# One more tile transposed on TensorE, and two loads of v moved within GpSimd's queue, in a fused retention and snake-MLP kernel

## Chip, cores and metric

The kernel runs on one core of a Trainium2 chip. The metric is the device time of one execution in microseconds (us). Before the change it is 214.4 us, the median of three runs (214.03, 214.40, 214.58).

## What is computed

There are two stages. The first is a retention recurrence over q, k and v, each 4 sequences x 8 heads x 768 positions x 64. Each head has a state of 64 x 64:

```
state = gamma[h] * state + outer(k[t], v[t])
y[t]  = (1/8) * q[t] @ state
```

Its output, as 3072 rows of 512, is the input x of the second:

```
h   = x @ w_in                         # 512 -> 2048
g   = h + sin(alpha*h)**2 / alpha
out = g @ w_out                        # 2048 -> 512
```

## The kernel before

**Tiles.** Time is cut into chunks of 128 positions, so that there are 24 tiles of 128 rows, six to a sequence. The list `P` (`order`, lines 47 and 48) is the order in which they are computed: first the first chunk of each of the four sequences (P[0] to P[3], also called e0 to e3), then the rest of sequence 0 (P[4] to P[8]), of sequence 1 (P[9] to P[13]), of 2 and of 3. From P[10] on tiles are "wide": their q, k and v come not in a chunk of their own but with all wide tiles of their sequence, in eight loads a tensor, one for each head (`load_seq`, line 89). P[4] to P[9] have loads of their own (`load_chunk`, line 73).

**What one tile needs.** (1) Its q and k in SBUF, and from them the transposed tile `qkT`. `stage_T` (line 236) makes it with eight transposes on TensorE into a PSUM tile and a copy out on VectorE or ScalarE. `turn` (line 248) makes it with one transposing DMA on SP's queue. (2) `stage_A`, for wide tiles `scores`: TensorE makes q·k scores from `qkT` in the PSUM buffer of the tag `pa`, of which there is one, and VectorE masks them. (3) `stage_M`, for wide tiles `inter` and `mix` (both called by `burst`): scores times v, plus q times the state, plus the new state. The v must have been scaled by decay factors (`scale_v`, line 133), for most tiles on GpSimd. (4) The result, one column block of `xT`, feeds the MLP.

**The MLP.** Tiles are taken in groups: four, then ten groups of two. In a `Slot` TensorE multiplies two of the 16 blocks of w_in with a group's `xT` into a PSUM tile `ph` (line 420, tag `mm`, four buffers), ScalarE takes the sine (423) and mostly the square (428), VectorE adds both into `gT` (435). `ff_out` (line 442) multiplies `gT` of the group before with w_out (445), `take` copies the result out of PSUM and SP stores it (460).

**Order of the work.** It is written out by hand; each engine takes its instructions in the order of the program. Up to line 742 it is a list of calls: the first group's MLP with tiles P[4], P[5] and the transposes of P[6] in between. Then `phase` (line 558) runs phases 1 to 10, one for each later group, eight slots each. In each slot it first issues the slot's products, then the attention steps that a table has for this place, then a share of the group before. A place is (phase, slot): `score` and `blend` say where a tile's scores and its mix are issued, `turns` where its transposing DMA is. Places matter to SP only as the order of its queue: an instruction there waits for its own data and holds all that come behind it.

**GpSimd's queue** (lines 629 to 658) holds the loads of q, k and v, which change fp32 to bf16 on the way, and the scalings of v, in the order of the text. A load also waits, before it is issued, for the landing of the one issued eight places before. The scaling of a tile stands behind all loads above it, and waits for its own load.

Of the kernel before, what the change touches and what calls it, by code (L numbers as in the profile page):

```python
# [15 lines left out]
def kernel(  # L16
# [15 lines left out]
    nc = tc.nc  # L32
# [3 lines left out]
    NJ = B * NCH  # L36
# [32 lines left out]
    def chunk_of(t, j):  # L69
        b, c = divmod(j, NCH)  # L70
        return t[b, :, c * C:(c + 1) * C, :].rearrange("h s d -> s h d")

    def load_chunk(j, names="qkv"):
        for name, src in (("q", q), ("k", k), ("v", v)):
            if name not in names:
                continue
            if name == "v":
                t = big.tile([128, H, D], BF16, name="vr", tag="vr", bufs=10)
            else:
                if ("qk", j) not in raw:  # L80
                    raw["qk", j] = big.tile([128, 2, H, D], BF16, name="qkr", tag="qkr", bufs=9)
                t = raw["qk", j][:, "qk".index(name)]
            nc.gpsimd.dma_start(out=t, in_=chunk_of(src, j))  # L83
            raw[name, j] = t

    def wide(j):
        return j >= NCH + 2 and j % NCH > 0

    def load_seq(bt, names="qkv"):

        cs = [c for c in range(NCH) if wide(bt * NCH + c)]
        nh = 2 * len(cs)
        if "q" in names:
            raw["seq", bt] = (big.tile([128, nh, 2, NP, D], BF16, name=f"qk_seq{bt}"),
                              big.tile([128, nh, NP, D], BF16, name=f"v_seq{bt}"))
        tqk, tv = raw["seq", bt]
        for name, src in (("q", q), ("k", k), ("v", v)):
            if name not in names:
                continue
            for h in range(H):  # L100
                r = slice(64 * (h // NP), 64 * (h // NP) + 64)
                o = tv[r, :, h % NP, :] if name == "v" else tqk[r, :, "qk".index(name), h % NP, :]
                nc.gpsimd.dma_start(out=o, in_=src[bt, h, cs[0] * C:, :].rearrange("(f i) d -> i f d", i=64))  # L103
        for i, c in enumerate(cs):
            j, f = bt * NCH + c, slice(2 * i, 2 * i + 2)
            raw["qk", j], raw["k", j], raw["v", j] = tqk[:, f], tqk[:, f, 1], tv[:, f]
# [26 lines left out]
    def scale_v(j, eng):  # L133
        t, by = raw["v", j], kg
        if wide(j):
            t, by = t.rearrange("i f p d -> i (f p) d"), kgq
        eng.tensor_mul(t, t, by[:, j % NCH, :, None].to_broadcast([128, H, D]))  # L137
# [98 lines left out]
    def stage_T(j, eng=None, tag="ty"):  # L236
        pt = psum.tile([128, 2 * NP, 128], BF16, name="pt", tag=tag, bufs=4 if tag == "mm" else 1)
        st["qkT", j] = work.tile([128, 2 * NP, 128], BF16, name="qkT", tag="qkT", bufs=6)
        for i in range(2):
            for p in range(NP):  # L240
                nc.tensor.transpose(pt[:, i * NP + p, :],
                                    raw["qk"[i], j][:, 2 * p:2 * p + 2, :].rearrange("p h d -> p (h d)"), ident)
        if eng is nc.scalar:
            nc.scalar.copy(st["qkT", j], pt)
        else:
            nc.vector.tensor_copy(st["qkT", j], pt)
# [36 lines left out]
    def stage_M(j, tag="ty"):  # L283
        c = j % NCH
        g, i = place[j]
        if g not in xT:
            xT[g] = work.tile([128, KS, sizes[g] * C], BF16, name="xT", tag="xT", bufs=3)
        qkT, aT, vs = st["qkT", j], st["aT", j], raw["v", j]
        py = psum.tile([128, NP, 128], F32, name="py", tag=tag)
        if c > 0:  # L290
            for p in range(NP):
                for e in range(2):
                    r = slice(64 * e, 64 * e + 64)
                    nc.tensor.matmul(py[r, p, :], s_bd[c % 2][:, p, r], qkT[:, p, :],
                                     start=(p == 0), stop=True, skip_group_check=True)
        for p in range(NP):
            for e in range(2):
                nc.tensor.matmul(py[64 * e:64 * e + 64, p, :], vs[:, 2 * p + e, :], aT[:, e, p, :],  # L298
                                 start=(c == 0 and p == 0), stop=True, skip_group_check=True)
        x = xT[g][:, :, i * C:(i + 1) * C]  # L300
        if c == 0:
            nc.scalar.copy(x, py)
            return
        ps = stage_S(j) if c < NCH - 1 else None
        nc.vector.tensor_mul(x, py, qg[:, c])
        if ps is not None:
            keep_S(j, ps)
# [187 lines left out]
    P = order  # L495
    e0, e1, e2, e3 = P[:B]
# [133 lines left out]
    load_chunk(P[8], "qk")  # L630
    load_chunk(P[7], "v")
    load_chunk(P[9], "qk")
    scale_v(P[6], nc.gpsimd)
    load_seq(1, "q")
    load_chunk(P[8], "v")
    scale_v(P[7], nc.gpsimd)
    load_chunk(P[9], "v")
    load_seq(1, "k")
    scale_v(P[8], nc.gpsimd)
    scale_v(e1, nc.gpsimd)  # L640
    scale_v(P[9], nc.gpsimd)
    load_seq(1, "v")
    scale_v(e2, nc.gpsimd)
# [96 lines left out]
    F(2, 11, 16)  # L740
    stage_M(P[5])
    stage_T(P[6], nc.vector, "mm")
    score = {6: (1, 1), 7: (1, 4), 8: (2, 0), 9: (2, 2), 10: (2, 5)}
    blend = {6: (1, 4), 7: (1, 6), 8: (2, 2), 9: (2, 5)}
    for g in range(3, NG - 1):
        first = P.index(groups[g + 1][0])
        for i, n in enumerate((1, 5)):
            score[first + i + 1] = blend[first + i] = (g, n)
    turns = {7: (1, 0), 8: (1, 2), 9: (1, 4), 10: (2, 0), **{n + 2: score[n] for n in range(9, NJ - 2)}}
    atts = {g: {} for g in range(1, NG)}  # L750

    def at(place, fn):
# [61 lines left out]
```

## Time and profile before

| | |
|---|---|
| median of the runs shown | 214.4 us |
| profiled execution | 214.89 us |
| its span, first to last instruction | 213.1 us |
| TensorE (PE) busy | 202.5 us, 95% |
| ScalarE (ACT) busy | 159.2 us, 75% |
| VectorE (DVE) busy | 154.3 us, 72% |
| GpSimd (POOL) busy | 110.7 us, 52% |
| chain that ended last | PE 64%, DMA 21%, POOL 9% |
| granted TensorE clock | 1.0 |

The profile is of one execution; its times are counted from the span's first instruction. PE is the matrix products, PEld the loading of their stationary operand, which runs beside them. Products overlap each other and their ends are modelled, so where a piece of work ends is best read from where the next one starts. An instruction's idle time is that of its engine just before it, with what ended it. A DMA is told by its issue and by the time from there to its landing. The chain of work that ended last is followed back from the last instruction to whatever released each one.

### The profile page before, as it was taken

How to read it: one execution, taken by the hardware profiler on the slowest of the kernel's cores; microseconds unless marked ns; L12 is line 12 of the kernel's file. 1: busy time of each engine (PE TensorE's matmuls, PEld its weight loads, DVE VectorE, ACT ScalarE, POOL GpSimd, SP SyncE). 2: the span in 40 equal slices, each digit the busy share in tenths (PEclk: the TensorE clock that was granted, in tenths of full speed). 3: DMA queues.
4: the chain of work that ended last, by engine and by line, in shares of the span. 5: the costliest groups of instructions: out<-in, count | busy, mean ns of one | idle time of the engine just before them, and what ended most of it. 6: DMA issues, size and time to landing. Idle time of an engine off the chain costs nothing.

```text
span 213.1 us, 5488 instructions
## 1 busy us (share of the span) xinstructions
PE 202.5 (95%) x2187; PEld 132.9 (62%) x2187; DVE 154.3 (72%) x350; ACT 159.2 (75%) x343; POOL 110.7 (52%) x148
## 2 busy tenths in 40 slices
PE   7758999999799999999999999999999999999994
PEld 2324644567566666766767667667667667666654
DVE  7589994876878678678678777777877877666550
ACT  6687898457688867977977977977876876788821
POOL 8899433896869839899989931001231131000000
PEclk9999999999999999999999999999999999999999
DMA  9999999999999999999999994407403100110112
GB/s 131 145 176 182 206 208 178 154 201 168 145 148 105 130 157 142 171 92 183 169 142 156 150 141 104 98 3 98 103 11 92 51 30 23 52 49 0 49 52 98
DMA packets 101337, 25.00 MB, mean 117 GB/s; under 512 B 93872, under 2 KB 98368, under 8 KB 101312
## 3 DMA queue, kind: packets, MB, share of 16 engines
q0 software_dynamic: 77504, 13.38, 87.5%
q1 hardware_dynamic: 23664, 11.22, 25.7%
q8 instruction: 17, 0.28, 0.6%
q14 instruction: 8, 0.07, 0.1%
q10 hardware_dynamic: 144, 0.07, 0.1%
HBM read 27.27 MB, written 6.29 MB: 157 GB/s over the span
## 4 chain that ended last, share of the span: by engine, by line
PE 64%; DMA 21%; POOL 9%; DVE 2%; ACT 2%; issue 1%; SPq 0%; POOLq 0%; DVEq 0%
PE po L445 30%; PE ph L420 27%; DMA w_out<-in_moe_w_out_dram 8%; DMA vr<-in_v_dram 4%; DMA qkr<-in_k_dram 4%; POOL qkr L83 3%; DMA qkT<-qk_seq 3%; DMA qk_seq<-in_k_dram 2%; PE poh L470 2%; POOL vr L83 2%; PE pa L332 2%; PE py L322 1%; ACT dec L164 1%; POOL w_out L116 1%; POOL qg L208 1%
## 5 line engine op out<-in xcount | busy, mean ns | idle before, releaser
L435 DVE SCALAR_TENSOR_TENSOR gT<-s,rec_alpha,ph 128x256 bf16<-128x256 f32 (+3 forms) x184 | 82.0, 488 | 38.0 <-ACT s L428 37.8
L423 ACT ACTIVATE s<-ph,alpha_sb 128x256 f32<-128x256 f32 (+3 forms) x184 | 79.3, 480 | 33.8 <-PE ph L420 32.2
L420 PE MATMUL ph<-xT,w_in 128*128 128x256 bf16 (+3 forms) x736 | 98.8, 277 | 0.7 <-DMA w_in<-in_moe_w_in_dram 0.4
L445 PE MATMUL po<-w_out,gT 128*128 128x512 bf16 x368 | 95.2, 380 | 0.2 <-DMA w_out<-in_moe_w_out_dram 0.2
L420 PEld LDWEIGHTS <-w_in 128*128 128x128 bf16 x736 | 70.6, 98 | 31.3 <-DMA w_in<-in_moe_w_in_dram 1.3
L428 ACT ACTIVATE s<-s 128x512 f32<-128x512 f32 (+1 forms) x91 | 56.4, 623 | 2.6
L445 PEld LDWEIGHTS <-gT 128*128 128x128 bf16 x368 | 34.0, 98 | 26.0 <-issue 0.5
L386 POOL CAST s_bd<-s_f 64x256 bf16<-64x256 f32 x10 | 4.0, 396 | 41.7 <-DVE s_f L379 23.6
L137 POOL TENSOR_TENSOR v_seq<-v_seq,kgq 128x512 bf16<-128x512 bf16 x14 | 14.7, 1070 | 10.5 <-DMA v_seq<-in_v_dram 5.5
L103 POOL DMA_DIRECT2D qk_seq<-in_k_dram x24 | 17.0, 730 | 3.1 <-DMA vr<-in_v_dram 1.4
L103 POOL DMA_DIRECT2D qk_seq<-in_q_dram x24 | 17.1, 743 | 2.6 <-DMA qkr<-in_k_dram 0.9
L457 DVE COPY o_sb<-po 128x512 f32<-128x512 f32 x19 | 13.1, 692 | 5.9 <-PE po L445 5.9
L103 POOL DMA_DIRECT2D v_seq<-in_v_dram x24 | 17.0, 752 | 0.0
L341 DVE TENSOR_TENSOR aTw<-pa,maskq 128x768 bf16<-128x768 f32 x14 | 13.3, 950 | 0.0
L83 POOL DMA_DIRECT2D vr<-in_v_dram x10 | 9.3, 929 | 3.3 <-DMA w_out<-in_moe_w_out_dram 3.0
L372 DVE TENSOR_TENSOR xT<-py,qg 128x256 bf16<-128x256 f32 x28 | 10.5, 416 | 0.0
L83 POOL DMA_DIRECT2D qkr<-in_k_dram x9 | 8.0, 887 | 4.0 <-DMA w_out<-in_moe_w_out_dram 3.2
L83 POOL DMA_DIRECT2D qkr<-in_q_dram x9 | 8.1, 898 | 3.8 <-DMA w_in<-in_moe_w_in_dram 3.7
L137 POOL TENSOR_TENSOR vr<-vr,kg 128x512 bf16<-128x512 bf16 x8 | 8.5, 1074 | 0.8 <-PE py L298 0.8
L489 PE MATMUL spare<-warm 128*128 128x512 bf16 x18 | 7.2, 521 | 1.2 <-DVE warm L147 1.2
L264 DVE TENSOR_TENSOR aT<-pa,mask 128x1024 bf16<-128x1024 f32 x6 | 7.3, 1220 | 0.9 <-PE pa L260 0.8
L281 ACT CAST s_bd<-ps 64x256 bf16<-64x256 f32 x14 | 5.1, 362 | 2.0 <-PE ps L274 1.9
(94 smaller groups left out, 151.8 us busy)
## 6 DMA issues: line engine op xcount, KB each, us to landing
out_dram<-o_sb SPq DMA_DIRECT2D x23, 256.0 KB, 2.9
w_in<-in_moe_w_in_dram POOLq DMA_DIRECT2D x4, 512.0 KB, 9.5
w_out<-in_moe_w_out_dram POOLq DMA_DIRECT2D x4, 512.0 KB, 13.0
vr<-in_v_dram POOLq DMA_DIRECT2D x10, 128.0 KB, 7.2
qk_seq<-in_q_dram POOLq DMA_DIRECT2D x16, 80.0 KB, 6.0
qk_seq<-in_k_dram POOLq DMA_DIRECT2D x16, 80.0 KB, 4.6
v_seq<-in_v_dram POOLq DMA_DIRECT2D x16, 80.0 KB, 6.1
qkr<-in_q_dram POOLq DMA_DIRECT2D x9, 128.0 KB, 7.2
```

The source lines that it names most:

```text
L83: nc.gpsimd.dma_start(out=t, in_=chunk_of(src, j))
L103: nc.gpsimd.dma_start(out=o, in_=src[bt, h, cs[0] * C:, :].rearrange("(f i) d -> i f d", i=64))
L137: eng.tensor_mul(t, t, by[:, j % NCH, :, None].to_broadcast([128, H, D]))
L264: nc.vector.tensor_mul(aT.rearrange("p e n t -> p (e n) t"), pa.rearrange("p e n t -> p (e n) t"), m)
L341: return {"mask": lambda: nc.vector.tensor_mul(aT, pa[:, :, 0:384].rearrange("p e (m t) -> p e m t", m=2), maskq[:, None, None, :].to_broa ...
L372: nc.vector.tensor_mul(x[:, 2 * b:2 * b + 2, :], py[b][:, 0:256].rearrange("p (m t) -> p m t", m=2), qg[:, c, 2 * b:2 * b + 2])
L420: nc.tensor.matmul(self.ph[:, m, :], w_in[:, i, f * 128:(f + 1) * 128], xT[g][:, i, self.lo:self.hi], start=(m == 0 and i == 0), stop=(i = ...
L423: nc.scalar.activation(out=self.s[:, m, :], in_=self.ph[:, m, :], func=ACTF.Sin, scale=alpha_sb[:, f:f + 1])
L428: nc.scalar.activation(out=self.s, in_=self.s, func=ACTF.Square)
L435: nc.vector.scalar_tensor_tensor(gT[self.g][:, f, self.lo:self.hi], self.s[:, m, :], rec_alpha[:, f:f + 1], self.ph[:, m, :], op0=ALU.mult ...
L445: nc.tensor.matmul(po[g, ts], gT[g][:, f, ts * C:(ts + 1) * C], w_out[:, f, :], start=(f == 0), stop=(f == FF - 1))
L457: nc.vector.tensor_copy(o_sb, po[g, ts])
```

## The change

P[7]'s `qkT` is made by `stage_T` on TensorE, right behind P[6]'s, into the PSUM buffer `pa`, with the copy out on ScalarE; its transposing DMA at place (1, 0) goes. Those of P[8] and P[9] move to (1, 0) and (1, 2), and P[10]'s from (2, 0) to (1, 7), which puts it ahead of the store of the first group's last tile on SP. In GpSimd's queue P[8]'s v is loaded ahead of P[6]'s scaling and of sequence 1's q; the scalings of P[7], e1 and P[8] follow that q, ahead of sequence 1's k; P[9]'s v is loaded behind this k, and its scaling comes next, ahead of sequence 1's v. The number of loads and scalings is the same.

```diff
     load_chunk(P[8], "qk")
     load_chunk(P[7], "v")
     load_chunk(P[9], "qk")
+    load_chunk(P[8], "v")
     scale_v(P[6], nc.gpsimd)
     load_seq(1, "q")
-    load_chunk(P[8], "v")
     scale_v(P[7], nc.gpsimd)
+    scale_v(e1, nc.gpsimd)
+    scale_v(P[8], nc.gpsimd)
+    load_seq(1, "k")
     load_chunk(P[9], "v")
-    load_seq(1, "k")
-    scale_v(P[8], nc.gpsimd)
-    scale_v(e1, nc.gpsimd)
     scale_v(P[9], nc.gpsimd)
     load_seq(1, "v")
     scale_v(e2, nc.gpsimd)
...
     stage_M(P[5])
     stage_T(P[6], nc.vector, "mm")
+    stage_T(P[7], nc.scalar, "pa")
...
-    turns = {7: (1, 0), 8: (1, 2), 9: (1, 4), 10: (2, 0), **{n + 2: score[n] for n in range(9, NJ - 2)}}
+    turns = {8: (1, 0), 9: (1, 2), 10: (1, 7), **{n + 2: score[n] for n in range(9, NJ - 2)}}
```

## The prediction

> **What bounds the kernel now.** I read the busy time of the engines by stretches first (us, then busy us of PE, PEld, DVE, ACT, POOL; clock; DMA):
>
> ```profile
> 45.00:55.00 10.00, 9.62 (x117) 6.80 (x115) 6.60 (x13) 7.70 (x18) 8.31 (x12) 1.00 1.95 176
> 55.00:65.00 10.00, 8.82 (x94) 6.21 (x95) 7.78 (x15) 7.66 (x19) 7.46 (x11) 1.00 2.45 148
> 65.00:75.00 10.00, 9.48 (x122) 6.35 (x121) 7.21 (x15) 8.27 (x19) 8.65 (x12) 1.00 1.29 119
> 75.00:85.00 10.00, 10.00 (x115) 6.86 (x114) 7.95 (x18) 6.71 (x15) 6.68 (x9) 1.00 1.12 145
> 85.00:200.00 115.00, 115.00 (x1343) 79.69 (x1341) 84.93 (x197) 91.91 (x195) 46.85 (x65) 1.00 0.85 91
> ```
>
> TensorE (PE) is never idle from 75 to 200 us, at the full granted clock, so whatever moves it at 75 us moves the end. In the 30 us before, it idles 0.38 + 1.18 + 0.52 = 2.08 us: all that this change can reach. TensorE's timeline says where (start, us, what, idle before it and what ended that):
>
> ```profile
> 46.62 0.62 PE L241 MATMUL pt<-ident,qkr 128*128 128x128 bf16 x8
> 47.42 0.38 PE L420 MATMUL ph<-xT,w_in 128*128 128x256 bf16 x2 [0.18 <-DVE xT L305]
> ...
> 54.51 0.29 PE L274 MATMUL ps<-vr,qkr 128*64 128x64 bf16 x8
> 56.18 0.40 PE L260 MATMUL pa<-qkT 64*128 64x128 bf16 x8 [1.38 <-DMA qkT<-qkr]
> ...
> 73.47 0.29 PE L274 MATMUL ps<-vr,qkr 128*64 128x64 bf16 x8
> 74.28 0.25 PE L332 MATMUL pa<-qkT 64*64 64x128 bf16 x4 [0.52 <-DMA qkT<-qk_seq]
> ```
>
> The 1.38 us are the scores of the eighth tile, P[7], which wait for its transposing DMA. The 0.52 us are the scores of P[10], the first wide tile; SP's timeline shows both transposes in its queue:
>
> ```profile
> 41.59 5.39 SPq L460 DMA_DIRECT2D out_dram<-o_sb  x3
> 47.16 8.63 SPq L251 DMA_TRANSPOSE qkT<-qkr  x3
> 63.48 0.34 SPq L460 DMA_DIRECT2D out_dram<-o_sb  x1
> 68.27 2.90 SPq L251 DMA_TRANSPOSE qkT<-qk_seq  x2
> ```
>
> P[7]'s is issued at 47.16, behind three stores, and lands 9.0 later (DMA issues of that stretch), 56.1. P[10]'s must wait for the sequence's last k head, as the chain of waits tells; above it, what GpSimd (POOL) did:
>
> ```profile
> 53.27 8.97 DMA vr<-in_v_dram
> 62.24 0.28 issue
> 62.52 0.68 POOL qk_seq L103
> 63.20 0.21 issue
> 63.41 4.55 DMA qk_seq<-in_k_dram
> ...
> 68.27 5.97 DMA qkT<-qk_seq
> ```
>
> ```profile
> 64.11 3.05 POOL L137 TENSOR_TENSOR vr<-vr,kg 128x512 bf16<-128x512 bf16 x3
> 67.10 5.49 POOL L103 DMA_DIRECT2D v_seq<-in_v_dram  x8
> ```
>
> So P[9]'s v (55.18) and P[8]'s v (53.27) lie in the queue ahead of the k heads, and each load waits for the one issued eight places before it: the seventh k head waits for P[8]'s v (62.24), the last for P[9]'s (63.1).
>
> **The change, part by part.**
>
> *Transposes of P[7] on TensorE.* Eight more (L241). The two earlier groups of eight in this stretch start at 38.17 and 40.99, and the work after them at 38.62 and 41.44: 0.45 each. After P[6]'s group the first slot could have started at 46.62 + 0.45 = 47.07, but started at 47.42, waiting for xT. So 0.35 of the new 0.45 lies in an idle time: slot at 47.52, **+0.10**. Their data are there: P[7]'s q and k, issued at 38.37 and 39.32, landed 6.8 and 6.4 later, 45.2 and 45.7, against 47.07. Their PSUM buffer (tag pa) was last read by the mask of P[5]'s scores, done at 44.21.
>
> *The copy on ScalarE (L244).* No row has 128x1024 on ACT. Copies of 256 and 512 columns take 0.36 (L281) and 0.57 (L232); ends 0.57 and 2 x 0.57 = 1.14; by the slope 0.57 + 2 x 0.21 = 0.99, which I take. ACT is free at 47.55 and idle until 48.49, so the copy runs from about 47.75 to 48.74, and the first sine starts at 48.74, 0.25 late (0.40 at 1.14). VectorE's adds follow: the second (L435, 51.95 to 52.81) ends at 53.06, and slot 4, which takes that add's PSUM buffer, is due at 53.07 + 0.10 = 53.17. Bounds 0 and 0.3; since VectorE is busy 4.88 of the 5 us from 50 to 55, I take **+0.10**, nearer to the free end. Later adds have their own idle time (0.77 before 56.62).
>
> *The wait of P[7]'s scores goes:* **-1.38**. They run at about 54.9 from a tile that has been ready since 48.8. Late next would be P[7]'s scaled v, for its mix at 59.23 - 1.3 = 57.9: its scaling now follows the eight q heads, 54.3 to 55.4. P[8]'s and P[9]'s transposes each move up one place on SP (the first waits for P[8]'s k, landed at 48.1); with the durations of before, 9.0 to 10.6, they land by about 59 and 63; needed at 62.63 and 67.11 less 1.3.
>
> *GpSimd's order.* P[8]'s v is issued at 45.1 instead of 53.27, which moves P[6]'s scaling (used at 54.0) and the q heads by 0.9. The seventh q head waits for P[9]'s k (landed 52.2), the eighth now for P[8]'s v, queued one chunk behind. A chunk is 1024 rows, and the queue alone moved 7332 packets in the 6 us from 37 to 43: 0.84, or twice that beside a transpose, 53.0 to 53.9. Eighth q head done by 54.3; three scalings, 3.05 as at 64.11: 57.4; eight k heads at 0.68 each, the last issued at 62.1, not 63.41. Each waits for the q head eight places before it, issued 10.3 to 8.5 earlier; the q heads of before landed 6.5 to 9.0 after issue. It lands 2.5 (the first v head, at 67.10, into an emptied queue) to 4.6 (as before) later, 64.6 to 66.7, against 67.97. P[10]'s transpose then lands at 5.97 as before: 70.9 to 73.0. TensorE wants it at 74.28 - 0.52 - 1.38 + 0.20 = 72.58. The bounds leave a wait of 0 to 0.5; I take 0, as the removed transpose also relieves the queue: from 55 to 61 it moved 3053 packets beside 2019 of the transposes, where it moves 7330 alone. **-0.52.**
>
> *P[10]'s transpose ahead of a store on SP.* The store of the first group's last tile waits until about 65 instead of 63.48. Its buffer is wanted three stores later, at 87: nothing.
>
> *P[9]'s v behind k.* Issued at about 62.8. Its scaling now stands ahead of the v heads on GpSimd, and holds them. The queue is nearly empty by then: 2.5 + 0.42 for twice the rows + 0.2 for the longer issue = 3.1; 3.6 with k heads still in it, landing at 66.4 (the least that a v load shows in this trace is 4.7, the ones near here 7 to 9). Scaled at 67.75, wanted at 71.7. The v heads start at 67.75 instead of 67.10, and P[10]'s scaled v, ready at 79.36 before, at 80.0; its mix (L349, at 82.05) wants it at 82.05 - 1.70 = 80.35. Nothing, with 0.3 to spare.
>
> **Sum:** 1.38 + 0.52 - 0.10 - 0.10 = 1.70. The profiled execution took 214.89 (span 213.1 and 1.8 around it): 213.2. The median of the runs shown is 214.4, 0.5 below it: **212.7**.
>
> [...]
>
> **Rivals.**
> - *One wait comes back in part.* P[10]'s transpose at 73.0, or its scaled v some tenths late: every tenth beyond the due time is a tenth lost. 213.1 to 214.1. For it: 0.3 to spare on one, bounds that straddle the due time on the other.
> - *The transposes were not the limit.* If the k heads land as late as before (67.97: heads bound by the queue and not by their issue), P[10]'s scores start at 74.28 again and swallow all that was gained: 214.4. Against it: a chunk and a transpose fewer ahead of them.
> - *Slower: GpSimd held by P[9]'s v.* With the 8.0 that this load took before, it lands at 70.8, its scaling ends at 72.15, the v heads start 5.05 late, P[10]'s v is scaled at 84.4, and the mix at 82.05 moves by 2.35: 216.8. It costs something from a landing at 66.7 on, and the kernel is slower than before from 68.45 on (5.65 after issue). Against it: before, two transposes and a full queue stood beside that load; now the heads ahead of it are paced by their issue.
>
> **Numbers.** Forecast 212.7 (212.3 to 213.1): 0.58. Part lost: 0.23. No change: 0.08. Slower, middle 215.5: 0.11. About 0.3% (0.64 us) is what a measurement can tell here. Faster: 0.58 + 0.18 of the part lost = 0.76; same 0.05 + 0.08 = 0.13; slower 0.11. The range takes in the forecast and the part lost: 212.2 (full 1.9 without the knock-on, less half the spread of the runs, 0.3) to 214.0.
>
> **What would show it.** Right: no idle time before L260 at 54.9; P[10]'s scores (L332) near 72.6 without a wait; GpSimd's k heads from 57.4 to 62.8; v heads from about 67.7; TensorE busy throughout from 73 on. Wrong: a wait for qkT at L332, a wait of L349 for P[10]'s v near 80 us, or slot 4 of phase 1 waiting for an add.

## The result and the profile after

Over 20 runs of each the changed kernel takes 213.21 us (median), the kernel before 214.31. The ratio is 0.9939, with a 95% interval of 0.9917 to 0.9961: a gain of 1.3 us, between 0.8 and 1.8. The forecast gain of 1.70 lies in that interval, near its upper end; 213.21 lies in the range of 212.2 to 214.0, though not in the forecast's own band of 212.3 to 213.1. The medians differ by 1.10 and not by 1.3 because the ratio leaves out two slow runs of the changed kernel (215.77 and 216.96), without which its median is 212.98.

The profiled execution of the changed kernel took 214.12 us, more than its median, with a span of 212.3. The stretches (us, busy us of PE, PEld, DVE, ACT, POOL; granted clock; DMA) show where the time of this one execution went:

```profile
0.00:45.00 45.00, 40.00 (x294) 20.36 (x294) 34.59 (x87) 32.64 (x73) 32.19 (x43) 0.92 1.68 173
45.00:55.00 10.00, 10.00 (x126) 7.30 (x125) 6.50 (x12) 7.54 (x18) 7.46 (x11) 1.00 1.79 166
55.00:65.00 10.00, 10.00 (x123) 7.01 (x121) 9.03 (x18) 9.11 (x21) 9.87 (x13) 1.00 2.22 123
65.00:75.00 10.00, 10.00 (x127) 6.75 (x126) 6.99 (x14) 8.27 (x19) 7.47 (x10) 1.00 1.42 160
85.00:200.00 115.00, 115.00 (x1341) 79.55 (x1340) 85.13 (x197) 91.70 (x195) 47.25 (x65) 1.00 0.84 90
```

TensorE's 2.08 us of idle time between 45 and 75 us are gone, all of them. What this execution lost lies ahead of the change: a mean granted clock of 0.92 in the first 45 us, where the profile of before has 1.00. The page's row of the clock, in 40 slices of 5.3 us, has it in the third and fourth slice:

```profile
PEclk9967999999999999999999999999999999999999
```

TensorE's timeline of the changed kernel at the three places that the prediction showed of before:

```profile
47.75 1.07 PE L241 MATMUL pt<-ident,qkr 128*128 128x128 bf16 x16
48.65 1.04 PE L420 MATMUL ph<-xT,w_in 128*128 128x256 bf16 x8
...
55.74 0.29 PE L274 MATMUL ps<-vr,qkr 128*64 128x64 bf16 x8
55.97 0.40 PE L260 MATMUL pa<-qkT 64*128 64x128 bf16 x8
...
73.25 0.29 PE L274 MATMUL ps<-vr,qkr 128*64 128x64 bf16 x8
73.48 0.25 PE L332 MATMUL pa<-qkT 64*64 64x128 bf16 x4
```

No line has an idle time behind it any more. The transposes of P[6] start at 47.75 instead of 46.62, 1.13 later, most likely for that clock; P[10]'s scores start at 73.48 instead of 74.28, 0.80 earlier. In between 1.93 us have gone, in this pair of executions: by the starts, P[7]'s scores come 1.44 and P[10]'s 0.58 sooner after the row ahead of them, and the first slot 0.10 later. To read every time below against the prediction's, add 1.13 to the latter.

GpSimd's timeline:

```profile
54.81 0.68 POOL L103 DMA_DIRECT2D qk_seq<-in_q_dram  x1 [2.12 <-DMA vr<-in_v_dram]
55.50 3.04 POOL L137 TENSOR_TENSOR vr<-vr,kg 128x512 bf16<-128x512 bf16 x3
58.49 5.49 POOL L103 DMA_DIRECT2D qk_seq<-in_k_dram  x8
63.90 0.98 POOL L83 DMA_DIRECT2D vr<-in_v_dram  x1
67.53 1.03 POOL L137 TENSOR_TENSOR vr<-vr,kg 128x512 bf16<-128x512 bf16 x1 [2.66 <-DMA vr<-in_v_dram]
68.53 5.50 POOL L103 DMA_DIRECT2D v_seq<-in_v_dram  x8
...
78.74 1.04 POOL L137 TENSOR_TENSOR v_seq<-v_seq,kgq 128x512 bf16<-128x512 bf16 x1 [3.64 <-ACT s L423]
```

The k heads now follow each other without a wait, 5.49 for eight, where the DMAs before them held them in the kernel before. SP's timeline shows what comes of it: P[10]'s transposing DMA is issued at 66.15, and by the DMA issues of that stretch it lands at 69.22, 4.3 us before TensorE asks for it.

```profile
48.53 6.26 SPq L251 DMA_TRANSPOSE qkT<-qkr  x2
66.15 1.24 SPq L251 DMA_TRANSPOSE qkT<-qk_seq  x1
67.49 0.52 SPq L460 DMA_DIRECT2D out_dram<-o_sb  x1
```

### The profile page after: what moved, and what is told of

It is laid out like the page before. It is cut to its first block, busy times and chain, and to the rows that moved or that the text cites. A ratio compares the mean times of both kernels' runs of the same rounds, so it can differ in the third digit from the quotient of the medians.

```text
span 212.3 us, 5502 instructions
## 1 busy us (share of the span) xinstructions
PE 204.3 (96%) x2195; PEld 134.2 (63%) x2195; DVE 154.3 (73%) x350; ACT 159.9 (75%) x344; POOL 110.6 (52%) x148
## 4 chain that ended last, share of the span: by engine, by line
PE 92%; DVE 3%; ACT 2%; issue 0%; POOL 0%; POOLq 0%; DVEq 0%
PE ph L420 39%; PE po L445 39%; PE pa L260 2%; PE poh L470 2%; PE pa L332 2%; PE py L298 1%; PE py L322 1%; DVE aT L264 1%; ACT dec L164 1%; PE spare L489 1%; PE py L294 1%; PE pt L241 1%; PE py L361 1%; PE py L349 1%; DVE gT L435 1%; PE ps L274 1%
## 5 line engine op out<-in xcount | busy, mean ns | idle before, releaser
L420 PE MATMUL ph<-xT,w_in 128*128 128x256 bf16 (+3 forms) x736 | 99.8, 279 | 0.0
L372 DVE TENSOR_TENSOR xT<-py,qg 128x256 bf16<-128x256 f32 x28 | 10.5, 416 | 0.0
L489 PE MATMUL spare<-warm 128*128 128x512 bf16 x18 | 7.9, 563 | 1.2 <-DVE warm L147 1.2
```

What stands on the lines that cost most here:

```text
L372: nc.vector.tensor_mul(x[:, 2 * b:2 * b + 2, :], py[b][:, 0:256].rearrange("p (m t) -> p m t", m=2), qg[:, c, 2 * b:2 * b + 2])
L420: nc.tensor.matmul(self.ph[:, m, :], w_in[:, i, f * 128:(f + 1) * 128], xT[g][:, i, self.lo:self.hi], start=(m == 0 and i == 0), stop=(i = ...
L489: nc.tensor.matmul(spare["ps"], warm[:, :128], warm, start=True, stop=True)
```

## Experiments

The theory after the result: two waits of TensorE went, P[7]'s by the transposes and P[10]'s by the moved loads, less 0.1 for the transposes. Rivals: one half alone does it; the waits of the one profile of before were longer than usual; the new work costs more than the 0.1.

Executions differ ahead of the change as well (in the first 46 us), so in the profiles I compare the stretch from P[6]'s transposes to the end of the span. The times of the runs are told with the ratio to the kernel of before, measured beside them.

**Each half alone.** The transposes, with the transposing DMAs at their new places, GpSimd's queue as before:

```diff
     stage_T(P[6], nc.vector, "mm")
+    stage_T(P[7], nc.scalar, "pa")
-    turns = {7: (1, 0), 8: (1, 2), 9: (1, 4), 10: (2, 0), ...
+    turns = {8: (1, 0), 9: (1, 2), 10: (1, 7), ...
```

> The changed kernel without the moves in GpSimd's queue: P[7] is transposed on TensorE, the transposing DMAs stand as in the changed kernel, the loads and scalings as before. Both theories: the idle time before P[7]'s scores (1.38 us in the profile of before) is gone, eight transposes cost 0.1. They differ on the first wide tile, P[10]. Theory (the moved loads are needed for the second wait): the last k head, still behind P[9]'s v, lands at about 67.5, its transpose at 73.5, TensorE is there at 72.6 and waits 0.9; the gain on before is 0.8 to 1.0 us. Rival (one transposing DMA fewer frees the queue by itself): last k head at 66.2, no wait, and the gain is that of the changed kernel, 1.2 to 1.8 us.

Measured: 213.60, ratio 0.9939 (0.9913 to 0.9965), that of the whole change, as the rival had it. P[10]'s scores do not wait in its profile: the last k head lands at 64.6. In the profile of before that reaches P[6]'s transposes at the same time (the second one, below) it lands at 65.9, so the transposing DMA that is gone probably did free the queue; but that profile has no wait there either. And TensorE waits at two other places:

```profile
55.79 1.03 PE L420 MATMUL ph<-xT,w_in 128*128 128x256 bf16 x8 [0.45 <-DVE gT L435]
...
61.20 1.03 PE L420 MATMUL ph<-xT,w_in 128*128 128x256 bf16 x8 [0.51 <-DVE xT L305]
```

Both are waits for VectorE, which has no idle time between them. Its timeline, and GpSimd's at the same time, have the reason: a square (L430) that takes 0.69 elsewhere takes 2.39 beside P[7]'s scaling:

```profile
52.44 2.39 DVE L430 TENSOR_TENSOR s<-s 128x512 f32<-128x512 f32 x1
54.87 1.66 DVE L435 SCALAR_TENSOR_TENSOR gT<-s,rec_alpha,ph 128x256 bf16<-128x256 f32 x4
```

```profile
52.30 0.90 POOL L83 DMA_DIRECT2D vr<-in_v_dram  x1 [0.78 <-DMA qk_seq<-in_q_dram]
53.22 1.05 POOL L137 TENSOR_TENSOR vr<-vr,kg 128x512 bf16<-128x512 bf16 x1
```

The moves in GpSimd's queue alone are the other half of the diff:

> The moves in GpSimd's queue alone; P[7] by its transposing DMA and all of these at the places of before. Theory: the wait before P[7]'s scores stays at 1.4 us or grows (P[8]'s v, 0.84 us of the queue, now runs beside that transpose), the one of P[10] shrinks from 0.5 to 0: gain 0 to 0.5 us on before. Rival (the queue's order is what counts): a gain of over 0.7 us, as P[7]'s transpose lands earlier too.

Measured: 214.56, ratio 1.0005 (0.9976 to 1.0033): no gain. In its profile P[10]'s scores do not wait, and P[7]'s wait 0.31 where the theory had 1.4 or more; but this execution reaches P[6]'s transposes only at 49.02, 2.4 us later than the profile of before, with its loads less late, so its waits need not be those of a usual one. Again a square is stretched, to 2.60, beside the three scalings, and 0.24 and 0.51 of waiting for VectorE come in. The queue's order by itself is worth nothing that can be measured; of these two halves the gain goes with the transposes.

**The price of the transposes.** Eight more of them behind the new ones, their result unused:

```diff
     stage_T(P[7], nc.scalar, "pa")
+    more = psum.tile([128, 2 * NP, 128], BF16, name="more", tag="ty")
+    for i in range(2):
+        for p in range(NP):
+            nc.tensor.transpose(more[:, i * NP + p, :], <q or k of P[7]>, ident)
```

> The changed kernel with eight more transposes of P[7] right behind the eight new ones, their result unused: the price of eight where no idle time covers them. Theory: 0.45 us more on TensorE, the first slot of phase 1 that much later, and the time 0.45 above the changed kernel's, as no wait is left to absorb it. [...] Second rival (slack in later waits absorbs it): no difference to the changed kernel.

Measured: 213.71, ratio 0.9953 (0.9921 to 0.9984). TensorE's timeline of its profile:

```profile
46.19 1.07 PE L241 MATMUL pt<-ident,qkr 128*128 128x128 bf16 x16
47.10 0.61 PE L747 MATMUL more<-ident,qkr 128*128 128x128 bf16 x8
47.54 1.04 PE L420 MATMUL ph<-xT,w_in 128*128 128x256 bf16 x8
```

The first slot starts 1.35 after P[6]'s transposes instead of 0.90, and the stretch is 165.1 us long instead of 164.6; the fastest run, 213.01, is 0.45 above the changed kernel's 212.56. So eight cost 0.45 where nothing covers them, and no later wait absorbs it: the theory holds. One transpose takes 0.22 in the trace, and they overlap: the eight that start at 47.10 are followed by the slot's first product at 47.54.

**The kernel of before again**, twice:

> The kernel of before itself, for a second profile of it and for the error of the comparison. Ratio 1.00. Theory (the two waits are as long in every execution): again about 1.4 us before P[7]'s scores and 0.5 before P[10]'s, 1.9 in all. Rival (the profiled execution of before had longer waits than the median one, which explains a gain of 1.1 to 1.3 where 1.7 was forecast): 0.9 to 1.5 us in all.

> The kernel of before once more, for a third profile of its waits. Of the first two, one had 1.38 us before P[7]'s scores and 0.52 before P[10]'s, the other 1.18 and none. Theory (the second wait is there in some executions only, and that is what the forecast's sum had too much): 1.1 to 1.4 and 0 to 0.3. Rival (0.5 is usual): over 0.4 before P[10]'s scores.

Measured: 214.84, ratio 0.9997 (0.9972 to 1.0022); and one run of 216.09. In the first profile TensorE waits 1.18 before P[7]'s scores and not at all before P[10]'s:

```profile
55.55 0.40 PE L260 MATMUL pa<-qkT 64*128 64x128 bf16 x8 [1.18 <-DMA qkT<-qkr]
```

In the second:

```profile
56.24 0.40 PE L260 MATMUL pa<-qkT 64*128 64x128 bf16 x8 [1.06 <-DMA qkT<-qkr]
...
75.50 0.25 PE L332 MATMUL pa<-qkT 64*64 64x128 bf16 x4 [1.67 <-DMA qkT<-qk_seq]
```

The first of the two fits its rival (1.18 in all). The second fits neither theory nor rival well: the wait before P[10]'s scores is over 0.4, but 0.5 is not usual. It is 0.52, 0 and 1.67 in three profiles of the same program. The wait before P[7]'s, 1.38, 1.18 and 1.06, is steadier.

**The place of P[10]'s transposing DMA.** `10: (1, 7)` back to `10: (2, 0)`:

> The changed kernel with P[10]'s transposing DMA back at place (2, 0), behind the store of the first group's last tile. Theory (the place is worth nothing: that store has its data at about 63 us, and the last k head lands at 65.9 in the changed kernel's profile): no idle time before P[10]'s scores, the time of the changed kernel, ratio to before about 0.994. Rival (the place brought the second wait's end): a wait of 0.5 us comes back, ratio about 0.996.

Measured: 213.15, ratio 0.9944 (0.9923 to 0.9965), no wait before P[10]'s scores. The place is worth nothing that can be measured, as forecast.

**P[7] turned by its DMA, but earlier.** GpSimd's queue as changed, no eight transposes:

```diff
     stage_M(P[4])
+    turn(P[7])
     F(2, 11, 16)
...
-    stage_T(P[7], nc.scalar, "pa")
```

> The changed kernel without the eight transposes on TensorE: P[7] is turned by its DMA again, but this is issued by hand ahead of SP's third store, right behind P[4]'s mix; the other transposing DMAs and GpSimd's queue as in the changed kernel. Theory (only the landing counts): issued at about 45.9 as soon as P[7]'s k has landed, landing 7.5 to 9.0 later at 53.4 to 54.9, TensorE there at 54.8: a wait of 0 to 0.3, against the 0.1 that eight transposes cost; ratio as the changed kernel's, 0.993 to 0.996. Rival (it is the transposing DMA's load on the queue that has to go): the q and k heads come some 1.7 us later, P[10]'s wait is back, ratio over 0.997.

Measured: 214.65, ratio 1.0009 (0.9983 to 1.0035): the gain is gone. Yet neither mechanism was the one: the DMA, issued at 45.27, lands at 53.5 in time for P[7]'s scores at 54.3, and P[10]'s do not wait. TensorE's, VectorE's and GpSimd's timelines of its profile:

```profile
61.60 1.03 PE L420 MATMUL ph<-xT,w_in 128*128 128x256 bf16 x8 [1.63 <-DVE xT L305]
```

```profile
57.26 2.77 DVE L430 TENSOR_TENSOR s<-s 128x512 f32<-128x512 f32 x1
60.07 0.87 DVE L435 SCALAR_TENSOR_TENSOR gT<-s,rec_alpha,ph 128x256 bf16<-128x256 f32 x2
60.86 0.69 DVE L305 TENSOR_TENSOR xT<-py,qg 128x512 bf16<-128x512 f32 x1
```

```profile
55.74 0.68 POOL L103 DMA_DIRECT2D qk_seq<-in_q_dram  x1 [2.65 <-DMA vr<-in_v_dram]
56.43 3.04 POOL L137 TENSOR_TENSOR vr<-vr,kg 128x512 bf16<-128x512 bf16 x3
```

P[8]'s v, issued at 44.52, lands beside that DMA at 55.07, after 10.5 us; in the run before this one it was issued at 43.86 and took 8.7, to 52.56. The eighth q head waits for it, so the three scalings start at 56.43 and meet VectorE's second square, which ends 0.56 after the last of them. In the changed kernel they run from 55.50 to 58.54, between the squares at 54.00 and 58.91: free by 0.4 us.

**Away with the squares.** If these meetings were what lifts half of the changed kernel's runs over its floor of 212.6, fewer scalings in between, or no squares on VectorE, should bring the median to the floor. Two edits of the changed kernel, each by itself:

```diff
     scale_v(P[7], nc.gpsimd)
-    scale_v(e1, nc.gpsimd)
-    scale_v(P[8], nc.gpsimd)
     load_seq(1, "k")
     load_chunk(P[9], "v")
+    scale_v(P[8], nc.gpsimd)
+    scale_v(e1, nc.gpsimd)
```

```diff
-    phase(1, out_pieces(0, (3,)), atts[1], 2, (2, 5))
+    phase(1, out_pieces(0, (3,)), atts[1], 2)
```

> The changed kernel with the scalings of P[8] and e1 behind P[9]'s v load instead of ahead of the k heads, so that one scaling instead of three lies between VectorE's two squares of phase 1. Theory (a scaling on GpSimd that runs beside such a square stretches it from 0.69 to 1.7 to 2.6 us, as the profiles of the two halves show, and TensorE then waits up to 1.0; this is where runs of the changed kernel above its floor of 212.6 come from): fewer such runs, median 212.7 to 212.9 where the changed kernel's was 213.2, ratio 0.990 to 0.992. Rival (the spread comes from the first 45 us): ratio as the changed kernel's, 0.994.

> The changed kernel with the two squares of phase 1 that VectorE takes (slots 2 and 5) on ScalarE: nothing that GpSimd's scalings could stretch is left there. Theory of the stretched squares: median 212.6 to 212.8, hardly a run above 213. Rival (ScalarE is the next bound: 9.1 of the 10 us from 55 to 65 are busy, and two squares are 1.26 more): TensorE waits for adds, 0.3 to 1.0 us slower than the changed kernel's floor, median 213 to 213.6. Rival (the spread comes from the first 45 us): median as the changed kernel's, 213.2.

Measured: 213.22, ratio 0.9942 (0.9923 to 0.9962), and 212.92, ratio 0.9938 (0.9915 to 0.9960); of the 12 runs of each, 8 and 6 still lie between 212.9 and 214.6. This theory of the spread falls. The stretches say where the spread is instead:

| profile | P[6]'s transposes start | span | from there to the end |
|---|---|---|---|
| changed kernel | 47.75 | 212.3 | 164.6 |
| P[10]'s turn back | 46.20 | 210.8 | 164.6 |
| two scalings later | 46.21 | 210.8 | 164.6 |
| squares on ScalarE | 46.87 | 211.5 | 164.6 |
| eight more transposes | 46.19 | 211.3 | 165.1 |
| transposes alone | 46.19 | 212.1 | 165.9 |
| queue alone | 49.02 | 214.9 | 165.9 |
| P[7]'s DMA earlier | 46.20 | 212.4 | 166.2 |
| before, three profiles | 46.62, 46.20, 47.00 | 213.1, 211.9, 214.3 | 166.5, 165.7, 167.3 |

In the four profiles of the changed kernel and its near kin the rest of the kernel takes the same 164.6; they differ only in when it starts. All of the spread that these show comes from the first 46 us.

The same edit of the squares was tried on three others:

> The run with P[7]'s transposing DMA ahead of SP's third store (no eight transposes; GpSimd's queue as changed), now with phase 1's two squares of VectorE on ScalarE. Its profile had TensorE idle 1.63 us at 61.6, behind VectorE, whose square at 57.26 took 2.78 us beside three scalings on GpSimd. Theory (the stretched square is the whole loss): the idle time goes, the floor is that of the changed kernel less 0.1 (212.5), median 212.6 to 213.2, ratio 0.993 to 0.995. Rival (it is the later loads, and another wait takes the place): the ratio stays at 0.998 to 1.001.

Measured: 214.37, ratio 0.9991 (0.9958 to 1.0025). The rival holds: the waits for VectorE are gone, and another has come, as TensorE's and GpSimd's timelines show:

```profile
83.42 0.25 PE L349 MATMUL py<-aTw,v_seq 64*64 64x128 bf16 x4 [1.38 <-POOL v_seq L137]
```

```profile
66.90 0.98 POOL L83 DMA_DIRECT2D vr<-in_v_dram  x1
70.65 1.03 POOL L137 TENSOR_TENSOR vr<-vr,kg 128x512 bf16<-128x512 bf16 x1 [2.77 <-DMA vr<-in_v_dram]
71.64 5.49 POOL L103 DMA_DIRECT2D v_seq<-in_v_dram  x8
...
82.32 1.04 POOL L137 TENSOR_TENSOR v_seq<-v_seq,kgq 128x512 bf16<-128x512 bf16 x1 [4.13 <-DMA v_seq<-in_v_dram]
```

This is the end that the prediction's slower rival has, v heads late and P[10]'s mix waiting for the scaled v, but not its cause. P[9]'s v lands 3.7 after its issue, nearly as in the changed kernel (3.55), and holds GpSimd for 2.77 (2.66 there); it is issued 3.0 later. The eighth q head is issued 3.0 later too, behind P[8]'s v. Counted from P[6]'s transposes, GpSimd's work from that head to P[9]'s v comes 2.8 later than in the changed kernel, and 2.5 later in the run without this edit: in both, P[7]'s DMA is in the queue.

> The transposes on TensorE alone (GpSimd's queue of before), with phase 1's two squares of VectorE on ScalarE. In its profile without that, the square at 52.44 took 2.39 us beside P[7]'s scaling, and TensorE waited 0.45 and 0.51 us for VectorE; P[10]'s scores did not wait. Theory (the moved queue is worth only that the scalings miss the squares): both waits go, median 0.2 to 0.5 below the run with the squares on VectorE, 212.7 to 213.2, ratio 0.991 to 0.994. Rival (the moved queue is needed for the second wait): a wait of 0.3 to 0.9 before P[10]'s scores, no gain over the transposes alone.

Measured: 214.19, ratio 0.9982 (0.9952 to 1.0012), against 0.9939 with the squares on VectorE. The theory fails here, and what the transposes alone are worth becomes uncertain: with the squares on ScalarE the whole change keeps its gain (0.9938) and the transposes alone do not, though the two intervals for the transposes alone overlap. The profile has none of the waits for VectorE, and only 0.18 before P[10]'s mix; its stretch is 165.0, so after P[6]'s transposes it does not show where the runs lose time. TensorE reached P[6]'s transposes at 47.0 to 47.9 in this profile and the three measured with it, and at 46.2 to 46.9 in the four before those; but the kernel of before had the same median beside both (214.46 and 214.47). Whether the first 46 us, a wait in other executions, the moved queue or chance is behind it stays open.

> The kernel of before with phase 1's two squares of VectorE on ScalarE, no other edit: what the squares' place is worth by itself. Theory (in before TensorE waits for P[7]'s transposing DMA whatever VectorE does): ratio 0.998 to 1.000, 1.2 to 1.4 us before P[7]'s scores still. Rival (stretched squares cost in before too): ratio below 0.997.

Measured: 214.30, ratio 0.9989 (0.9959 to 1.0018): no gain to speak of, as the theory had it. But its one profile has no wait for either transposing DMA, where the theory had 1.2 to 1.4: P[5]'s mix was held, and P[7]'s transpose was in time.

```profile
46.40 0.41 PE L294 MATMUL py<-qkT,s_bd 128*64 128x128 bf16 x8 [0.83 <-DVE xT L305]
```

So the first wait need not be in every execution either; the stretch is 164.4.

## Why the prediction was right, and where it was off

- **Transposes, +0.10: right.** From P[6]'s transposes to the first slot 0.90 instead of 0.80. Uncovered, eight cost 0.45, as read from the profile of before.
- **Copy on ScalarE, 0.99: right (1.01).** The knock-on of 0.10 at slot 4 did not come: TensorE has no idle time there.
- **P[7]'s wait, -1.38: right in kind**, and the part that most likely carries the gain: the transposes alone reach the ratio of the whole (0.9939), the queue alone reaches none. Against it stands the variant with the squares on ScalarE (0.9982). Three profiles of before have 1.38, 1.18 and 1.06, one of its kin none.
- **GpSimd's order: right in its times.** With 1.13 added, the last k head was to be issued at 63.2 (63.23), to land 2.5 to 4.6 later (2.7: 65.91); P[9]'s v to be issued at 63.9 (63.90) and to land 3.6 later (3.55: 67.45); the v heads to start at 68.9 (68.53); P[10]'s v to be ready at 81.1 (79.8). The mix asks for it at 81.25: 1.5 to spare, where I had 0.3. The v heads started 0.35 sooner, and from there the scaled v took 1.0 less than before; that P[10]'s transposing DMA was out of the way by then is a likely reason, not tested.
- **P[10]'s wait, -0.52: the term that was mis-sized.** I took one execution's number for the program's. It is 0.52, 0 and 1.67. The bounds for the landing were off too: 72.0 to 74.1 with 1.13 added, by the 5.97 of before; it took 3.07 and landed at 69.22. Nor is it shown that the moved loads were needed: the profiles of the transposes alone have no such wait either, but one of before has none as well.
- **The sum.** Between the profile that the prediction read and the changed kernel's the stretch shrank by 1.9 (166.5 to 164.6), more than 1.70. Against the other two profiles of before it is 1.1 and 2.7. The runs give 1.3 (0.8 to 1.8). The fastest runs, 213.49 and 212.56, differ by 0.93, about what P[7]'s wait alone explains. How often before has which sum, three profiles can't tell; that the forecast came out inside the interval is partly luck.
- **The rivals.** The median of 213.21 lies in the band of the first (one wait comes back in part), but in the profile no wait came back: what was short is the wait that before loses. The second did not happen: the last k head landed 3.2 sooner than before, counted from P[6]'s transposes. Nor did the third (GpSimd held by P[9]'s v); its end came in a variant, at 1.38, from another cause. What I did not see at all is that the scalings' new place lies 0.4 us from a square of VectorE, whose meeting costs up to 1.6: no row of before showed it, though the second profile of before has one (1.73 at 52.30, beside a scaling).

No version tried here is measurably faster than the changed kernel; 212.92 with the squares on ScalarE has an interval that covers its ratio.

## What to carry to other kernels

A wait on a DMA, read from one profile, is one draw (0.52, 0 and 1.67 here): take two or three profiles before its length goes into a sum, and let its lower bound be zero. When a load or an engine's helper work is moved, list what it will run beside at its new place, the engine that this case's squares and scalings show it to hold up above all (a square of 0.69 took up to 2.77), not only who waits for its result. A transfer taken off a full queue may be worth more for what it lets pass than for its own wait: P[7]'s transposes on TensorE cost 0.1, and three attempts to keep its DMA in the queue gained nothing, in two of them (by one profile each) though that DMA landed in time.

## What the runs showed of the hardware

- **VectorE's square waited for GpSimd's scalings.** In four profiles the square (L430, 128x512 fp32, in place) met a scaling on GpSimd and took 1.73, 2.39, 2.60 and 2.77 instead of 0.69. In all four it ended 0.56 after the end of the last scaling, and it waited through one that had not begun when it did: the later ones of three (2.60 and 2.77), or the only one, which began 0.12 later (1.73) and 0.78 later (2.39). VectorE's masks and adds, with one operand in PSUM, were not stretched: in the changed kernel a mask at 57.00 takes 1.22 beside the scalings, as elsewhere, and in the run with P[7]'s DMA earlier two adds at 56.48 take 0.87, against 0.86 to 0.88 elsewhere. The other way round there is one case: a scaling of the queue-alone run that began at 46.71, inside a scaling that VectorE did from 46.52 to 47.20, took 1.38, where the same scaling takes 1.08 or 1.09 in the other profiles. Why the two squares that began 0.12 and 0.78 before the scaling were held nevertheless is open: both began beside a load's issue on GpSimd (at 51.50 and 52.30, 0.90 each), but a square of the changed kernel beside the issues of k heads (58.91) took 0.69.
- **Transposing DMAs beside loads were dear.** From 55 to 61 us of the kernel before, 3053 packets of the loads passed beside 2019 of the transposes, where 7332 pass alone in as long a time: the 4279 missing are, as an estimate (4279 of 7332, times 6 us), 3.5 us of the loads' queue for about two transposes.
- **The granted clock fell once, to 0.50 for 6.8 us**, from 12.2 to 19.0 us of the changed kernel's profile, at a place that the change does not touch. That execution reached P[6]'s transposes 1.13 us later than the profile of before. The clock falls without the change too: over the whole execution it is 0.984 here, and 0.984 also in a run of the kernel of before (214.94).
